# Decoding float64 weights in an attention, experts and SwiGLU kernel: the sign bit cleared on ScalarE, and one epsilon addition for two heads

## Chip, cores and metric

The kernel is one program on one core of a Trainium2 chip. The metric is the device time of one execution in microseconds (us). Lower is better. Three executions were timed without a profiler, and one more was profiled.

## What is computed

Three layers stand behind each other; the first two shapes are (4, 8, 576, 64) per head and (2304, 512) per token.

```python
q_s = softmax(q, axis=-1)                 # with 1e-9 added to each sum
k_s = exp(k - max(k, axis=2)); k_s = k_s / (sum(k_s, axis=2) + 1e-9)
attn = q_s @ (k_s^T @ v)                  # per batch and head
x = attn as (2304, 512)
p = domain_probs / (sum(domain_probs) + 1e-9)
x = sum over e of p[:, e] * (relu(x @ w1[e]) @ w2[e])         # 4 experts, 512 -> 1024 -> 512
out = (silu(x @ w_gate) * (x @ w_val)) @ w_out                # 512 -> 1536 -> 512
```

The three weights of the last layer arrive as float64; everything else is float32. The kernel turns the float64 words into float32 by integer and float operations on their two 32-bit halves, which is called the decode below.

## The kernel before, in words

**Tiling.** The 2304 tokens are worked in two halves, and each half in two blocks X (512 tokens) and Y (640 tokens). A step is one unit of 256 hidden columns for one block. An expert step makes the hidden tile `g` of its unit with seven products instead of eight, each product three matmuls on a high and a low part (`mm3`, L109 to L111, output tiles `h`), turns it into a high and a low part `hh` (ScalarE, L638) and `hl` (VectorE, L643), and in the next step multiplies it with the second weight into tiles `o` of 128x512 (L693 to L695), which VectorE adds to the running sum `acc` (L704). Between the seven products, banks are copied out by ScalarE (`sn`, L503) and combined by VectorE (L509, L518, L524). `weave` lays the `o` tiles between the products.

**What lies between the steps.** In the steps of the first half, attention for batches 2 and 3 runs as a generator (`attend`) on a PSUM bank of its own, "at": column maxima (`ktp`, `mx`, `kmb`), the product of keys and values (`kvp`), transposes of the queries (`qtp`, split into `qT` on ScalarE and VectorE by L104 and L105) and their product `x`. All of these tiles take turns in the bank "at", so that a later one waits until the earlier one has been read. Around the 500th microsecond the kernel turns from the first half to the second.

**The decode.** 36 pieces of 128x512 numbers (`DEC`), two buffers `r` in turn. `decode_load` (L548) loads a piece, 17 positions (about two steps) ahead of its use. `decode` has three stages, placed every two positions: L558 on ScalarE turns the low words into float; L559 on VectorE masks the sign bit off the high words and writes the copy `c`; L561 clamps `c` as float32; then L563 shifts, L564 puts the sign back, L566 adds the low part; the result is stored to DRAM and loaded again when its step comes.

**The attention's key side.** `att_kv` ends with the product `kvp` of 128 rows (two heads of 64) by 130 columns: for each of the two heads 64 columns of values and one column of ones, which gives the sum over the keys. L236 adds epsilon to this sum for the 64 rows of each head, L237 takes the reciprocal, L240 and L241 scale by it. It is called 16 times, with 32 instructions of L236.

**What sets the order.** From step 2 on, the instructions of TensorE and ScalarE stand in the order in which the code is written (`ordered`). Those of VectorE, GpSimd and of the queue of transfers (SyncE) are put in order by a scheduler that works with estimated times; so is everything ahead of step 2. Each engine then works through its list strictly in order.

Of the kernel before, what the change touches and what calls it, by code (L numbers as in the profile page):

```python
# [10 lines left out]
F32 = mybir.dt.float32  # L11
# [3 lines left out]
AF = mybir.ActivationFunctionType  # L15
ALU = mybir.AluOpType
# [3 lines left out]
EPS = 1e-9  # L20
# [7 lines left out]
def attention_experts_swiglu(ctx: ExitStack, tc: tile.TileContext, q, k, v, probs, w1, w2, wg, wv, wo, out):  # L28
# [12 lines left out]
    nc = tc.nc  # L41
    B, H, S, D = q.shape
# [13 lines left out]
    GH = 2  # L56
# [20 lines left out]
    def sbt(tag, shape, name, dt=F32):  # L77
        return sb.tile(shape, dt, tag=tag, name=name, bufs=BUFS[tag])
# [4 lines left out]
    def ps(tag, name):  # L83
        if tag in TURNS:
            TURNS[tag].append(TURNS[tag].pop(0))
            tag = TURNS[tag][0]
        return psp[-1].tile([P, 512], F32, tag=tag, name=name, bufs=BUFS[tag])
# [12 lines left out]
    def f32(ap):  # L100
        return ap.bitcast(F32)
# [15 lines left out]
    def store_later(dst, src):  # L117
        later.append((now[0], dst, src))
# [57 lines left out]
    def load_q(b, g, qt):  # L176
        h = slice(g * GH, (g + 1) * GH)
        nc.sync.dma_start(qt, q[b, h, 0:SM, :].rearrange("h (p c) d -> p h c d", c=C))
        nc.sync.dma_start(rests[b, g][RQ], q[b, h, SM:S, :].rearrange("h r d -> r h d"))
        qin[b, g] = (qt, rests.pop((b, g)))  # L180
# [3 lines left out]
    def W(z):  # L184
        return WAITS[z]

    def att_kv(b, g, tag, tag_m, tag_kv, bank):


        nm = f"{b}{g}"  # L190
        kt, vt, kr, vr = kin.pop((b, g))
        m = sbt(tag_m, [P, 2, P], f"m{nm}")
        kc = kt.rearrange("p h c d -> p c h d")
        nc.vector.tensor_tensor(m.rearrange("p c (h d) -> p c h d", h=GH), kc[:, 0:2], kc[:, 2:4], ALU.max)
        yield W(0), False
        tp = ps(bank, f"ktp{nm}")[:, :2 * P + SR]
        for c in range(2):
            nc.tensor.transpose(tp[:, c * P:(c + 1) * P], m[:, c], ident)
        nc.tensor.transpose(tp[:, 2 * P:], kr[R].rearrange("p h d -> p (h d)"), ident[R, R])
        yield W(1), True  # L200
        mx = sbt("ti", [P, 1], f"mx{nm}")
        nc.vector.tensor_reduce(mx, tp, AX.X, ALU.max)
        yield W(2), False
        mb = ps(bank, f"kmb{nm}")[:, :P]
        nc.tensor.matmul(mb, mx.to_broadcast([P, P]), ident, start=True, stop=True)
        yield W(3), True
        es = sbt(tag, [P, 2, C, GH, D], f"e{nm}") if isinstance(tag, str) else tag
        ek, eqs[b, g] = es[:, 0], es[:, 1]
        mbv = mb.rearrange("p (h d) -> p h d", h=GH)
        nc.vector.tensor_tensor(  # L210
            ek.rearrange("p c h d -> p h c d"), kt, mbv[:, :, None, :].to_broadcast([P, GH, C, D]), ALU.subtract
        )
        nc.vector.tensor_tensor(kr[R], kr[R], mbv[R], ALU.subtract)
        if (b, g) in rests:
            load_q(b, g, kt)
        nc.scalar.activation(ek, ek, AF.Exp)
        nc.scalar.activation(kr[R], kr[R], AF.Exp)
        yield W(4), False
        o = ps(bank, f"kvp{nm}")[:, :GH * D1]
        for c in range(C):  # L220
            nc.tensor.matmul(  # L221
                o, ek[:, c].rearrange("p h d -> p (h d)"), vt[:, c].rearrange("p h d -> p (h d)"),
                start=c == 0, stop=False,
            )
        nc.tensor.matmul(
            o, kr[R].rearrange("p h d -> p (h d)"), vr[R].rearrange("p h d -> p (h d)"), start=False, stop=True
        )
        yield W(5), True
        rs = sbt("ti", [P, 1], f"rs{nm}")
        ov = o.rearrange("p (z e) -> p z e", z=GH)  # L230
        kk = sbt(tag_kv, [P, 2, P], f"kk{nm}", F32R)
        kh, kl = kk[:, 0], kk[:, 1]
        nc.gpsimd.memset(f32(kk), 0.0)
        for z in range(GH):
            zz = slice(z * D, (z + 1) * D)
            nc.vector.tensor_scalar_add(rs[zz], ov[zz, z, D:], EPS)  # L236
        nc.vector.reciprocal(rs, rs)  # L237
        for z in range(GH):
            zz = slice(z * D, (z + 1) * D)
            nc.scalar.activation(kh[zz, zz], ov[zz, z, 0:D], AF.Copy, scale=rs[zz])  # L240
            nc.vector.scalar_tensor_tensor(kl[zz, zz], ov[zz, z, 0:D], rs[zz], f32(kh)[zz, zz], ALU.mult, ALU.subtract)  # L241
        kvs[b, g] = (kh, kl)
        yield W(6), False
# [89 lines left out]
    def attend(groups, bank):  # L333
# [4 lines left out]
        def softmaxes():  # L338
            for z, (b, g) in enumerate(groups):
                while done[0] < z - 1:  # L340
                    yield 1, False
                load_kv(b, g, "kv", "rs")
                yield 4, False
                for wait in att_kv(b, g, "kv", "sm", "sm", bank):
                    yield wait
                for wait in att_q(b, g, nc.vector):
                    yield wait
                done[1] += 1
# [204 lines left out]
    def decode(n):  # L553
        what, f, z = DEC[n]
        r = r64.pop(n)
        rv = r[:, 0:2 * NE].rearrange("p (n b) -> p n b", b=2)
        lo, hi, c = rv[:, :, 0], rv[:, :, 1], r[:, 2 * NE:]
        nc.scalar.activation(lo, lo.bitcast(U32), AF.Copy, scale=2.0 ** -29)  # L558
        nc.vector.tensor_scalar(c, hi, 0x7FFFFFFF, None, ALU.bitwise_and)  # L559
        cf = c.bitcast(F32)  # L560
        nc.vector.tensor_scalar(cf, cf, LEAST, MOST, ALU.max, ALU.min)  # L561
        yield
        nc.vector.tensor_scalar(c, c, 3, 0x3FFFFFF8, ALU.logical_shift_left, ALU.bitwise_and)  # L563
        nc.vector.scalar_tensor_tensor(c, hi, -0x40000000, c, ALU.bitwise_and, ALU.bitwise_or)  # L564
        yield
        nc.vector.tensor_tensor(c, c, lo, ALU.add)  # L566
        if (what, f) not in w32:
            w32[what, f] = dram.tile([P, 2 * NE], F32, tag=f"w32_{what}{f}", name=f"w32_{what}{f}")
        store_later(w32[what, f][:, z * NE:(z + 1) * NE], cf)
        yield  # L570
# [212 lines left out]
    if True:  # L783
# [41 lines left out]
        def start(n):  # L825
            dec[n] = decode(n)
            next(dec[n])
# [6 lines left out]
        for n in range(len(DEC)):  # L834
            z = DEC0 + n * DEC1
# [151 lines left out]
        for b in range(2):  # L987
            for g in range(G):
                chains[f"K{b}{g}"] = att_kv(b, g, e_of[b][g], "sn", kk_of[b][g], kv_bank[b][g])
                chains[f"Q{b}{g}"] = att_q(b, g, QENG[b * G + g])  # L990
                for z in range(2):
                    xb = kv_bank[0][g % 2 * 2 + z] if b == 0 else ("at", "hB")[z]
                    chains[f"X{b}{g}{z}"] = att_x(b, g, z, xb, b == 0)
# [42 lines left out]
```

## Time and profile before

| what | value |
|---|---|
| median of three timed executions | 1337.72 us (1336.94 to 1338.19) |
| profiled execution, its own time | 1339.92 us |
| span of the profiled execution, first to last instruction | 1338.1 us |
| TensorE busy | 1284.3 us, 96% |
| VectorE busy | 966.3 us, 72% |
| ScalarE busy | 598.1 us, 45% |
| GpSimd busy | 562.8 us, 42% |
| mean granted TensorE clock | 0.983 of full speed |

The profiled execution took 1.8 us more than its span, which lies ahead of the first and behind the last instruction. Busy shares are means over stages with different limits. PE is TensorE, DVE is VectorE, ACT is ScalarE, POOL is GpSimd and SPq the queue that issues transfers; PEclk is the granted TensorE clock as a share of full speed; Lnnn is a line of the kernel.

### The profile page before, as it was taken

Reading aid. Unit: us, or ns where it says so; the run is one execution under the profiler, and the core shown is the slowest. Engines: PE = TensorE matmul, PEld = TensorE weight load, DVE = VectorE, ACT = ScalarE, POOL = GpSimd, SP = SyncE. Lnnn points to the kernel's source line nnn. Section 1 sums busy time; section 2 is a strip of 40 time slices with the busy share of each in tenths; the row PEclk is TensorE's granted clock in tenths of the full one; section 3 lists DMA queues with packets and bytes.
Section 4 is the critical chain, followed back from the end, with each engine's and each line's share of the span. In section 5 each row is a group of like instructions: output and inputs, shape, how many; then the busy total and the mean of one; then the engine's idle time right before and its main releaser. Section 6 shows DMA issues by size and latency. Waiting matters only on the chain.

```text
span 1338.1 us, 20294 instructions
## 1 busy us (share of the span) xinstructions
PE 1284.3 (96%) x7568; PEld 1147.2 (86%) x7568; DVE 966.3 (72%) x1634; ACT 598.1 (45%) x1316; POOL 562.8 (42%) x587
## 2 busy tenths in 40 slices
PE   5889999999999998999999999999999999999998
PEld 3678888888888887888888888898988899999997
DVE  6886778778778889677787877555677766666665
ACT  4654334444344444434444343345444544444442
POOL 4753433443254435443545434353444444333420
PEclk9689999999999999999999999999999999999999
DMA  9311423433323334134444432463144247111102
GB/s 206 86 54 40 148 74 102 130 96 92 113 95 112 107 113 157 69 135 129 145 145 154 131 107 72 150 208 117 64 163 155 97 137 254 55 48 48 48 1 71
DMA packets 111298, 148.15 MB, mean 111 GB/s; under 512 B 30560, under 2 KB 71520, under 8 KB 111200
## 3 DMA queue, kind: packets, MB, share of 16 engines
q1 hardware_dynamic: 111200, 146.87, 34.8%
q8 instruction: 59, 0.97, 0.3%
q14 instruction: 39, 0.32, 0.1%
HBM read 109.09 MB, written 37.75 MB: 110 GB/s over the span
## 4 chain that ended last, share of the span: by engine, by line
PE 78%; DVE 10%; DMA 5%; ACT 2%; issue 2%; SPq 1%; POOL 1%; DVEq 0%; POOLq 0%; ACTq 0%
PE o L693 11%; PE o L695 11%; PE o L694 11%; PE h L109 7%; PE h L110 7%; PE h L111 7%; PE h_1g L109 2%; PE h_1g L111 2%; PE h_1g L110 2%; PE h_1v L109 2%; PE h_1v L110 2%; PE h_1v L111 2%; DMA r<-in_moe_w_gate_dram 2%; PE kvp L221 2%; PE h_0v L109 1%
## 5 line engine op out<-in xcount | busy, mean ns | idle before, releaser
L693 PE MATMUL o<-oh,hh 128*128 128x512 f32 x792 | 315.7, 399 | 3.0 <-DVE acc L704 1.5
L695 PE MATMUL o<-oh,hl 128*128 128x512 f32 x792 | 314.6, 397 | 2.5 <-DVE hl L643 2.3
L694 PE MATMUL o<-ol,hh 128*128 128x512 f32 x792 | 312.4, 394 | 0.0
L704 DVE SCALAR_TENSOR_TENSOR acc<-o,pn,acc 128x512 f32<-128x512 f32 x270 | 200.6, 745 | 73.2 <-PE o L695 72.5
L503 ACT COPY sn<-h 128x256 f32<-128x256 f32 (+1 forms) x192 | 76.2, 397 | 253.0 <-PE h L111 252.4
L695 PEld LDWEIGHTS o<-oh,hl 128*128 128x128 f32 x792 | 148.9, 188 | 39.6 <-DVE hl L643 4.2
L638 ACT ACTIVATE hh<-g 128x512 fp32r<-128x512 f32 (+1 forms) x176 | 119.4, 686 | 130.7 <-DVE g L524 73.5
L693 PEld LDWEIGHTS o<-oh,hh 128*128 128x128 f32 x792 | 149.1, 188 | 22.6 <-DVE acc L704 1.7
L694 PEld LDWEIGHTS o<-ol,hh 128*128 128x128 f32 x792 | 148.9, 188 | 17.2
L643 DVE SCALAR_TENSOR_TENSOR hl<-g,hh 128x512 fp32r<-128x512 f32 (+1 forms) x128 | 109.2, 855 | 31.5 <-ACT hh L638 28.7
L708 DVE TENSOR_TENSOR acc<-o,acc 128x512 f32<-128x512 f32 x90 | 61.9, 688 | 45.9 <-PE o L695 44.8
L521 ACT COPY g<-h 128x256 f32<-128x256 f32 (+1 forms) x64 | 25.6, 400 | 89.4 <-PE h L111 89.3
L645 DVE TENSOR_TENSOR hl<-g,hh 128x512 fp32r<-128x512 f32 (+1 forms) x48 | 48.6, 1012 | 3.2 <-ACT hh L638 2.4
L559 DVE TENSOR_SCALAR r<-r 128x512 int32<-128x512 int32 x36 | 23.1, 642 | 30.6 <-DMA r<-in_moe_w_val_dram 11.7
L105 POOL TENSOR_TENSOR xo<-xp,xo 128x256 fp32r<-128x256 f32 (+1 forms) x24 | 22.4, 935 | 52.5 <-ACT xo L104 47.2
L662 ACT ACTIVATE g<-g 128x512 f32<-128x512 f32 (+1 forms) x48 | 33.0, 688 | 21.0 <-DVE g L524 21.0
L524 DVE TENSOR_TENSOR g<-h,sn 128x256 f32<-128x256 f32 (+1 forms) x64 | 29.0, 453 | 17.9 <-PE h L111 17.5
L503 ACT COPY sn_1g<-h_1g 128x320 f32<-128x320 f32 x36 | 15.4, 427 | 56.2 <-PE h_1g L111 56.1
L518 DVE TENSOR_TENSOR g<-h,sn 128x256 f32<-128x256 f32 (+1 forms) x64 | 28.9, 451 | 9.7 <-ACT sn L503 9.5
L566 DVE CUSTOM_DVE_ANT_0 r<-r 128x1024 uint16<-128x1024 uint16 x36 | 32.0, 889 | 3.1 <-ACT r L558 3.0
L509 DVE TENSOR_TENSOR g<-h,sn 128x256 f32<-128x256 f32 (+1 forms) x64 | 28.8, 451 | 3.7 <-PE h L111 2.3
L564 DVE SCALAR_TENSOR_TENSOR r<-r 128x512 int32<-128x512 int32 x36 | 31.0, 862 | 0.7
(1174 smaller groups left out, 3857.1 us busy)
## 6 DMA issues: line engine op xcount, KB each, us to landing
pd<-xo SPq DMA_DIRECT2D x28, 320.0 KB, 2.8
pd<-xo SPq DMA_DIRECT2D x28, 256.0 KB, 2.5
r<-in_moe_w_gate_dram SPq DMA_DIRECT2D x12, 512.0 KB, 4.3
r<-in_moe_w_val_dram SPq DMA_DIRECT2D x12, 512.0 KB, 4.6
r<-in_moe_w_out_dram SPq DMA_DIRECT2D x12, 512.0 KB, 4.0
xl<-pd SPq DMA_DIRECT2D x14, 320.0 KB, 5.3
xh<-pd SPq DMA_DIRECT2D x14, 320.0 KB, 5.3
out_dram<-acc SPq DMA_DIRECT2D x16, 256.0 KB, 2.3
```

Source lines behind the costliest of these rows:

```text
L109: nc.tensor.matmul(o, wh, xh, start=first, stop=False, skip_group_check=more)
L110: nc.tensor.matmul(o, wh, xl, start=False, stop=False, skip_group_check=more)
L111: nc.tensor.matmul(o, wl, xh, start=False, stop=last, skip_group_check=more)
L503: nc.scalar.copy(sn[z], banks[0])
L638: nc.scalar.activation(hh[:, :, t * n:(t + 1) * n], g[:, :, t], AF.Relu if kind == "e" else AF.Copy)
L643: nc.vector.scalar_tensor_tensor(hl[:, :, ts], g[:, :, t], 0.0, f32(hh[:, :, ts]), ALU.max, ALU.subtract)
L645: nc.vector.tensor_tensor(hl[:, :, ts], g[:, :, t], f32(hh[:, :, ts]), ALU.subtract)
L693: nc.tensor.matmul(p, hh[:, z, ts], w[z][0], start=z == 0, stop=False)
L694: nc.tensor.matmul(p, hh[:, z, ts], w[z][1], start=False, stop=False)
L695: nc.tensor.matmul(p, hl[:, z, ts], w[z][0], start=False, stop=z == NF - 1)
L704: nc.vector.scalar_tensor_tensor(o, p, weight, o, ALU.mult, ALU.add)
L708: nc.vector.tensor_tensor(o, p, o, ALU.add)
```

## The change

Two edits. The mask of the sign bit, an integer operation on VectorE, becomes an absolute value on ScalarE: it reads the high words as float32 and writes the same copy `c`. And since each row of `kvp` holds its own key sum in the column of ones of either head, the two additions of epsilon on 64 rows become one on 128 rows, which reads the first head's column.

```diff
@@ att_kv
         nc.gpsimd.memset(f32(kk), 0.0)
-        for z in range(GH):
-            zz = slice(z * D, (z + 1) * D)
-            nc.vector.tensor_scalar_add(rs[zz], ov[zz, z, D:], EPS)
+        nc.vector.tensor_scalar_add(rs, ov[:, 0, D:], EPS)
         nc.vector.reciprocal(rs, rs)
@@ decode
         nc.scalar.activation(lo, lo.bitcast(U32), AF.Copy, scale=2.0 ** -29)
-        nc.vector.tensor_scalar(c, hi, 0x7FFFFFFF, None, ALU.bitwise_and)
         cf = c.bitcast(F32)
+        nc.scalar.activation(cf, hi.bitcast(F32), AF.Abs)
         nc.vector.tensor_scalar(cf, cf, LEAST, MOST, ALU.max, ALU.min)
         yield
```

Lines behind the first edit move up by two. In the changed kernel the decode reads: L556 low words and L558 absolute value, both ScalarE; L559 clamp, L561 shift, L562 sign, L564 addition, all VectorE (before: L561, L563, L564, L566). Likewise L704 becomes L702, L643 L641, L518 L516, L524 L522, L509 L507, L503 L501, L638 L636. L105 and L210 keep their numbers.

Through the scheduler the first edit also moves the rest of the decode on VectorE. The first place is VectorE's list around one of the eight column maxima of attention in the first half, the one whose bank "at" is freed by the VectorE read L105 `qT` (L210 is the first reader of the tile `kmb` that takes the bank next). Before:

```order
L704 SCALAR_TENSOR_TENSOR acc_68<-o_1_2_3595,pn,acc_68 128x512
L559 TENSOR_SCALAR r_1_1560<-r_1_1560 128x512
L561 TENSOR_SCALAR r_1_1560<-r_1_1560 128x512
L563 TENSOR_SCALAR r_1_1560<-r_1_1560 128x512
L564 SCALAR_TENSOR_TENSOR r_1_1560<-r_1_1560 128x512
L524 TENSOR_TENSOR g_0_3499<-h_01_3529,sn_02_3568 128x256
L105 TENSOR_TENSOR qT_3631<-qtp_3615,qT_3631 128x256
```

With the change, the same place:

```order
L702 SCALAR_TENSOR_TENSOR acc_68<-o_1_2_3582,pn,acc_68 128x512
L522 TENSOR_TENSOR g_0_3486<-h_01_3516,sn_03_3576 128x256
L641 SCALAR_TENSOR_TENSOR hl_0_3488<-g_0_3486,hh_0_3487 128x2x256
L105 TENSOR_TENSOR qT_3618<-qtp_3602,qT_3618 128x256
L702 SCALAR_TENSOR_TENSOR acc_68<-o_1_3_3605,pn,acc_68 128x512
L210 TENSOR_TENSOR e_3652<-kv_3432,kmb_3630 128x2x4x64
```

The four decode instructions of piece 11 (`r_1`) are gone from here. They now stand in VectorE's list about two steps later, behind piece 11's two instructions on ScalarE. Before, this second place held only the last of the five, L566:

```order
L643 SCALAR_TENSOR_TENSOR hl_0_3800<-g_0_3798,hh_0_3799 128x2x256
L704 SCALAR_TENSOR_TENSOR acc_68<-o_1_4_3921,pn,acc_68 128x512
L566 ISA r_1_1560<-r_1_1560 128x1024
L509 TENSOR_TENSOR g_1_3936<-h_12_3958,sn_11_3946 128x320
L105 TENSOR_TENSOR qT_3982<-qtp_3969,qT_3982 128x320
L704 SCALAR_TENSOR_TENSOR acc_67<-o_0_0_3985,pn,acc_67 128x512
```

With the change:

```order
L641 SCALAR_TENSOR_TENSOR hl_0_3786<-g_0_3784,hh_0_3785 128x2x256
L559 TENSOR_SCALAR r_1_1551<-r_1_1551 128x512
L702 SCALAR_TENSOR_TENSOR acc_68<-o_1_4_3907,pn,acc_68 128x512
L561 TENSOR_SCALAR r_1_1551<-r_1_1551 128x512
L507 TENSOR_TENSOR g_1_3922<-h_12_3944,sn_11_3932 128x320
L562 SCALAR_TENSOR_TENSOR r_1_1551<-r_1_1551 128x512
L105 TENSOR_TENSOR qT_3968<-qtp_3955,qT_3968 128x320
L564 ISA r_1_1551<-r_1_1551 128x1024
L702 SCALAR_TENSOR_TENSOR acc_67<-o_0_0_3971,pn,acc_67 128x512
```

All four instructions that the change leaves on VectorE stand together here, with other work between them. All 36 pieces move in this way. The third place is ScalarE's list at piece 25, where a bank copy stands right behind the decode. Before:

```order
L638 ACTIVATE hh_1_6712<-g_1_6711 128x2x320 x2
L558 ACTIVATE r_1_1560<-r_1_1560 128x512
L503 COPY sn_01_6837<-h_00_6830 128x256
L104 CAST xo_6840<-xp_6530 128x256
L104 CAST oh_6862<-raw22o 128x512
```

With the change:

```order
L636 ACTIVATE hh_1_6696<-g_1_6695 128x2x320 x2
L556 ACTIVATE r_1_1551<-r_1_1551 128x512
L558 ACTIVATE r_1_1551<-r_1_1551 128x512
L501 COPY sn_01_6821<-h_00_6814 128x256
L104 CAST xo_6824<-xp_6514 128x256
L104 CAST oh_6846<-raw22o 128x512
```

The absolute value stands between the low words and the bank copy. ScalarE's list has two table loads (ACT_TABLE_LOAD) in all, in both kernels and at the same two places.

## Rows read from the trace of the kernel before

**Rows 1.** Windows: length, busy us (count) of PE, PEld, DVE, ACT, POOL; PEclk, DMA.

```profile
140.00:480.00 340.00, 333.37 (x1932) 293.95 (x1931) 267.41 (x478) 145.41 (x319) 136.71 (x150) 0.99 0.35 107
480.00:540.00 60.00, 52.51 (x299) 45.63 (x298) 52.42 (x76) 28.86 (x59) 30.54 (x25) 0.97 0.42 135
540.00:840.00 300.00, 299.08 (x1738) 267.52 (x1737) 225.67 (x358) 128.56 (x276) 138.43 (x129) 1.00 0.38 122
```

**Rows 2.** Waits of PE, 130 to 480 us: total, times, longest.

```profile
PE kmb L205 <- DVE qT L105: 5.0, 2, 3.0
PE h L109 <- DVE g L518: 1.0, 2, 0.6
PE o L695 <- DVE hl L643: 0.3, 1, 0.3
```

**Rows 3.** Waits of PE, 480 to 540 us; last row: the one of 540 to 860.

```profile
PE o L695 <- DVE hl L643: 2.0, 1, 2.0
PE h L109 <- DVE g L518: 1.6, 2, 1.3
PE o L693 <- DVE acc L704: 1.5, 1, 1.5
...
PE h L109 <- DVE g L518: 0.7, 1, 0.7
```

**Rows 4.** Chain that ended last, 155.0 to 163.2 us: start, length, what.

```profile
155.60 4.56 DMA r<-in_moe_w_val_dram
...
160.26 0.43 DVE r L559
...
162.16 0.46 PE kmb L205 x2
```

**Rows 5.** The same chain, 339 to 351 us.

```profile
339.16 5.85 DMA r<-in_moe_w_out_dram
...
345.14 1.32 DVE r L559
...
348.36 0.69 DVE r L564
...
349.86 0.46 PE kmb L205 x2
```

**Rows 6.** Windows of 3.4 us: behind each stop, and one at full clock.

```profile
162.90:166.30 3.40, 3.40 (x14) 3.27 (x13) 2.22 (x5) 1.15 (x3) 0.00 (x0) 0.50 0.85 250
166.40:169.80 3.40, 3.40 (x22) 3.12 (x21) 2.61 (x6) 0.43 (x1) 0.00 (x0) 1.00 0.30 84
350.70:354.10 3.40, 3.40 (x14) 3.30 (x13) 2.41 (x5) 1.15 (x3) 0.00 (x0) 0.51 0.26 92
```

**Rows 7.** DVE groups by form, 130 to 860 us: busy, mean ns | idle before, releasers.

```profile
L559 DVE TENSOR_SCALAR r<-r 128x512 int32<-128x512 int32 x36 | 23.1, 642 | 30.6 <-DMA r<-in_moe_w_val_dram 11.7 <-DMA r<-in_moe_w_gate_dram 10.9 <-DMA r<-in_moe_w_out_dram 8.0
L566 DVE CUSTOM_DVE_ANT_0 r<-r 128x1024 uint16<-128x1024 uint16 x36 | 32.0, 889 | 3.1 <-ACT r L558 3.0
```

**Rows 8.** Instructions of three lines: duration ns min/median/max, first and last start.

```profile
L558 ACT ACTIVATE r<-r x36: 653/672/696, 151.8 to 832.1; 128x512 int32<-128x512 uint32 x36
L559 DVE TENSOR_SCALAR r<-r x36: 410/428/1524, 149.8 to 804.2; 128x512 int32<-128x512 int32 x36
L236 DVE TENSOR_SCALAR rs<-kvp x32: 140/156/164, 23.8 to 452.5; 64x1 f32<-64x1 f32 x32
```

**Rows 9.** Timeline of ACT and PE at pieces 25 and 14: start, length, [idle before].

```profile
654.92 0.67 ACT L558 ACTIVATE r<-r 128x512 int32<-128x512 uint32 x1
655.48 0.35 ACT L503 COPY sn<-h 128x256 f32<-128x256 f32 x1
657.36 0.28 PE L109 MATMUL h<-xh,wh22a 128*128 128x256 f32 x1
...
439.12 0.43 ACT L503 COPY sn<-h 128x320 f32<-128x320 f32 x1 [1.37 <-PE h L111]
```

**Rows 10.** Chain that ended last in the turn, 498 to 513 us.

```profile
502.07 0.56 ACT r L558
```

## The prediction

> **What bounds the kernel now.** I read first the busy time by stage. In the first half, TensorE is busy 333.4 of 340 us and VectorE 267.4; in the turn 52.5 of 60 and 52.4; in the second half 299.1 of 300 and 225.7 [rows 1]. So TensorE bounds, and only its idle time can be won. The waits of TensorE show where that idle time lies. From 130 to 480 us they come to 6.3 us, of which 5.0 are two stops of the matmul `kmb` behind VectorE's read of `qT` [rows 2]. The turn holds three waits on VectorE of 5.1 us together and some smaller ones, and from there to 860 us there is one of 0.7 us [rows 3]. Behind 860 us nothing is decoded, and the change moves nothing there.
>
> Next I read what VectorE was doing ahead of the two stops. The chain of waits says the same both times: a load of `r` lands, the mask L559 runs, then work that has nothing to do with it, then `qT`, then `kmb` [rows 4, 5]. L559 stands in VectorE's list ahead of `qT`, and its piece has not landed. The scheduler, it seems, took the load to be quicker than it is. Over all 36 pieces VectorE stood idle 30.6 us ahead of L559, every time on a load [rows 7]. Most of this costs nothing, because TensorE has other tiles to work on; twice it cost a stop.
>
> A stop costs more than its length. The granted clock in the 3.4 us behind each one is 0.50 and 0.51, the lower of the two levels (1.2 of 2.4 GHz), after TensorE had stood still for 2 and 3 us; just after, it is 1.00 again. In that stretch 14 matmuls start instead of 22 [rows 6]. Eight of 22 in 3.4 us is 1.2 us for each stop.
>
> **The change, part by part.**
>
> *The mask goes from VectorE.* 36 instructions, 23.1 us busy, and 30.6 us of waiting ahead of them [rows 7]. The busy time by itself is worth nothing where VectorE has slack. What counts is that the instruction which waits for the load leaves VectorE's list, and that the three behind it leave that place too: as the order shows, clamp, shift and sign now stand about two steps later, behind ScalarE's two instructions for the same piece. At the second stop the load lands at 345.0 us (339.16 + 5.85), and four decode instructions, from L559 to L564, then run until 349.05 [rows 5] ahead of the one that reads `qT`. With the change none stands there. At the first stop piece 2's mask and piece 1's burst are gone; piece 0's burst stands there in their stead, earlier, and has no load to wait for. So both stops go: 5.0 us of waiting and 2 x 1.2 us of slow clock, 7.4 us.
>
> The other waits outside the turn come to 1.0 + 0.3 + 0.7 = 2.0 us [rows 2, 3]. Some stand behind a decode burst and some behind VectorE's general load; bounds 0 and 2.0, I take half, 1.0.
>
> *The absolute value comes to ScalarE.* No absolute value was traced. The nearest row is L558, which reads the same buffer with the same step and writes 128x512: 672 ns [rows 8]; the bounds are its 653 and 696. 36 x 0.67 = 24.1 us on an engine that is busy 145 of 340 us in the first half [rows 1]. No table load is added. Its load is in the buffer long before: ScalarE comes to the last piece at 832.1 us, where VectorE's mask ran at 804.2 as soon as the load was there [rows 8]. If the addition L566, whose end frees the buffer for the next load, slips by the 3 us or so of the burst now ahead of it, those 28 us are hardly touched. Behind it on ScalarE stands whatever the step copies next. I went through all 36 places in the timeline: at 20 of them ScalarE idles over 0.67 us before its next instruction, as the 1.37 us at piece 14, and the absolute value fits in. At the other 16 the next instruction is pushed, up to 0.67 us, as at piece 25, where the copy L503 starts while L558 drains. There the copy ends at 655.83 and the product that needs its bank starts at 657.36 [rows 9], a lead of 1.5 us, so TensorE should not see it. Cost with that cover 0; without it 16 x 0.67 = 10.7 us.
>
> *The clamp now waits for ScalarE.* Behind it on VectorE stand bank reads such as L518 and evictions. How long it waits isn't in the trace; the nearest row is L566, which the scheduler placed behind L558 in the same manner, and which waited in 5 of 36 cases, 3.0 us in all [rows 7]. The bounds are 0 and 36 x 0.6 = 21.6 us of VectorE's time. I take about the 3.0 us that L566 now no longer pays: no difference.
>
> *The burst in its new place.* Four instructions of 0.4 to 1.5 us stand together ahead of an addition or a bank read. Before, three or four of them stood together as well, so the length is no news, only the place. Of the eight `kmb` places in the order, three have a burst within two steps ahead; the timeline of before has time to spare at two of them and almost none at the third. I take 0.7 us of new waits, between 0 and one whole new stop of 2.5 + 1.2 us.
>
> *The turn.* There the chain that ended last runs through L558 on ScalarE to the weight casts [rows 10], so one absolute value lies on the path: 0.7 us lost. Against it, shift and sign of piece 18 no longer stand ahead of the addition for which TensorE waited 1.5 us [rows 3]. Net 0.8 us won, between -0.7 and 5.1.
>
> *The epsilon.* 16 instructions of 156 ns go [rows 8], 2.5 us of VectorE. The instruction on 128 rows should take as long as that on 64, since the elements per row are the same. Most calls lie under TensorE's work; those of the start, where VectorE sets the pace, may give 0.3 us (0 to 2.5).
>
> **Sum.** 7.4 + 1.0 + 0.8 + 0.3 - 0.7 = 8.8 us. The profiled execution took 1339.9 us, which would become 1331.1. The median of the timed runs stands 2.2 us lower, at 1337.7; I take the same saving from it: 1328.9, so 1329.
>
> **The rivals.**
>
> *The turn opens too.* If all three waits on VectorE there go (5.1 us instead of 1.5), with a slow stretch of clock that follows one of them, and all of the 2.0 us outside, the gain is near 15 us: 1318 to 1325. For it: VectorE is at its fullest there, 52.4 of 60 us [rows 1]. Against it: what fills it there is the preparation of the next half, and that stays.
>
> *The wait comes back as a wait for ScalarE.* If every clamp waits 0.6 us, 21.6 of the 30.6 us are back, and by that measure 8.8 x 9.0 / 30.6 = 2.6 us of gain are left: 1335. Against it: L566 waited in 5 cases only.
>
> *ScalarE's copies come late.* If each of the 16 pushes reaches TensorE, 10.7 us eat the gain: 1339.6. Against it speaks the lead of 1.5 us. The Trainium skill, page "ScalarE: Activation LUTs", section "Rules for kernel authors", says that simple functions such as relu, max and min belong on VectorE and not on ScalarE. By that rule the move is a loss. The rows agree that the single instruction gets dearer (672 against 428 ns at the median [rows 8]), but which engine waits for what is not in the rule.
>
> *The burst stops `kmb` elsewhere* (the other sign). The same mechanism as now, at another place: a burst ahead of `qT`, TensorE standing still 2.5 us and 1.2 us of slow clock behind it, 3.7 us each. One or two such stops leave a gain; from four on, 14.8 us, the kernel is slower than before: 1343.7. For it: the two stops of now were as unforeseen. Against it: the bursts no longer begin with a load that is late.
>
> **How the numbers follow.** The forecast (1325 to 1333) gets 0.62, the open turn 0.10, the wait for ScalarE (1333 to 1338) 0.15, the late copies 0.05, the new stops 0.08. A measurement here can tell about 0.2%, 2.7 us, so faster means under 1335.0 and slower above 1340.4. Faster: 0.62 + 0.10 + 0.04 of the wait for ScalarE = 0.76. Slower: 0.07 of the new stops and 0.02 of the late copies = 0.09. The rest, 0.15, is no difference. The range goes from 1322, in the middle of the open turn, to 1337, in the upper part of the wait for ScalarE.
>
> **What would show it.** After the change the waits of TensorE from 130 to 480 us should hold no wait of `kmb` over 1 us, and no stretch at half clock there. VectorE should wait for no load of `r`; the clamp should wait for ScalarE a few microseconds in all. The absolute value should take 0.65 to 0.70 us. The turn should stay at 7 us of waits or so. The forecast is wrong if the start changes by more than 2 us, since the scheduler also reorders it and I have no row that prices that; if a new stop appears at one of the `kmb` places; or if the two stops belong to the profiled execution and not to the timed ones.

## The result, and the profile after

The changed kernel takes 1325.89 us (median of 4, 1324.73 to 1330.49) against 1337.45 us for the kernel before beside it (4 runs): a ratio of 0.9912 [0.9884, 0.9941], 11.6 us by the medians. A second measurement gave 0.9906 [0.9886, 0.9926]. The forecast was 1329.0 us, a gain of 8.8. By the profiled executions it is 14.0 us (1339.92 to 1325.93), but the one of before ran 2.5 us above its median, and the second profile of the changed kernel took 1328.14 us.

Windows of the changed kernel, with the columns of [rows 1]:

```profile
140.00:480.00 340.00, 338.95 (x1992) 300.54 (x1991) 258.44 (x462) 159.92 (x347) 140.75 (x156) 1.00 0.36 111
480.00:540.00 60.00, 54.27 (x311) 47.21 (x310) 50.27 (x71) 30.01 (x62) 28.85 (x24) 0.97 0.39 123
540.00:840.00 300.00, 300.00 (x1749) 269.12 (x1749) 227.06 (x349) 138.72 (x293) 142.74 (x134) 1.00 0.37 120
```

In the first half TensorE is idle for 1.0 us of 340 instead of 6.6 [rows 1], and starts 1992 matmuls in it instead of 1932. The second half has no idle time left. The turn is nearly as it was.

The waits of TensorE, 140 to 480 us (first row) and 480 to 540 us (the others), which answer to [rows 2, 3]:

```profile
PE o L691 <- DVE acc L702: 0.8, 1, 0.8
...
PE h L109 <- DVE g L516: 3.7, 2, 2.5
PE h L110 <- POOL xl L105: 0.8, 1, 0.8
PE o L693 <- DVE hl L641: 0.6, 1, 0.6
PE o L691 <- ACT xt L408: 0.6, 1, 0.6
```

Both stops of `kmb` are gone, and from 540 to 860 us no wait is left. (L691 was L693, L408 was L410.)

The chain that ended last, at the place of the second stop, 341.1 to 342 us:

```profile
341.11 0.16 PE h L110
341.27 0.46 PE kmb L205 x2
341.73 0.23 PE o L691
```

Where before a load, the mask and three more decode instructions led up to `kmb` [rows 5], the chain is now TensorE's own: `kmb` follows the matmul ahead of it without a gap. The clock stays up behind it; two windows of 3.4 us, behind either place of `kmb` (158.8 and 341.3 us):

```profile
158.90:162.30 3.40, 3.40 (x24) 3.23 (x23) 2.93 (x6) 1.58 (x4) 0.46 (x2) 1.00 0.83 236
341.30:344.70 3.40, 3.40 (x23) 3.27 (x24) 3.18 (x6) 1.52 (x4) 0.69 (x2) 1.00 0.46 125
```

24 and 23 matmuls at 1.00 stand where it was 14 at 0.50 and 0.51 [rows 6].

The instructions of the absolute value and the clamp (duration in ns: least, median, most; first and last start; who waited for them, us and times):

```profile
L558 ACT ACTIVATE r<-r x36: 641/660/678, 151.1 to 818.2; 128x512 f32<-128x512 f32 x36
  DVE r L559: 3.3, 10
...
L559 DVE TENSOR_SCALAR r<-r x36: 412/428/1532, 151.8 to 819.7; 128x512 f32<-128x512 f32 x36
```

**Where the gain lies.** ScalarE's conversion of the low words is the first instruction of each piece, its order on ScalarE is fixed from step 2 on, and it comes 36 times; its start times serve as landmarks. Its first and last starts were 151.8 and 832.1 us [rows 8] and are now:

```profile
L556 ACT ACTIVATE r<-r x36: 649/669/683, 150.6 to 817.7; 128x512 int32<-128x512 uint32 x36
```

So the kernel is 1.2 us ahead when the decode begins and 14.4 ahead when it ends. The table says in which stretch each kernel wins (minus) or loses time against the profiled execution of before: the shift of a landmark less that of the one before it. Piece 0 to 1 holds the first stop, 9 to 10 the second, 16 to 20 is the turn.

| us | start to 0 | 0 to 1 | 1 to 9 | 9 to 10 | 10 to 16 | 16 to 20 | 20 to 35 | 35 to end | sum |
|---|---|---|---|---|---|---|---|---|---|
| the change | -1.2 | -3.8 | -1.0 | -4.5 | -1.5 | -0.9 | -1.7 | +0.5 | -14.0 |
| the change again | -0.7 | -3.8 | -1.0 | -4.5 | -1.6 | +0.1 | -1.7 | +1.2 | -11.8 |
| sign only | -0.7 | -3.8 | -0.7 | -4.5 | -1.5 | -1.0 | -1.7 | +1.2 | -12.7 |
| epsilon only | +2.2 | -1.6 | +0.2 | -0.2 | -0.2 | +0.3 | +0.1 | +2.1 | +2.9 |
| mask behind ScalarE | -2.0 | -2.7 | -0.4 | -4.5 | -1.3 | -1.1 | +1.2 | +0.8 | -10.1 |
| mask and absolute value | -1.9 | -1.8 | -1.2 | -3.1 | -0.9 | -0.5 | -0.8 | 0.0 | -10.0 |
| absolute value twice | +0.6 | -3.3 | -0.6 | -4.5 | -1.0 | +0.1 | 0.0 | +0.7 | -7.9 |
| pieces 0 to 15 | -2.0 | -2.7 | -0.9 | -4.5 | -0.1 | +1.2 | -0.3 | +1.4 | -8.0 |
| pieces 16 to 35 | -2.3 | -1.6 | +1.0 | +0.1 | -1.0 | -0.9 | -1.7 | -0.2 | -6.6 |
| no sign at all | +3.0 | -2.0 | 0.0 | -0.6 | 0.0 | -0.9 | +0.8 | +0.2 | +0.4 |

Each row is one execution. The start moves by 5 us in all from kernel to kernel, in both directions. Where the change itself is run again, the stretches between the pieces repeat to 0.1 us outside the turn; the turn differs by 1.0 us and the end by 0.7.

### The profile page after: what moved, and what is told of

Its sections match the earlier page's. It is cut to its first block, busy times and chain, and to the rows that moved or that the text cites. A ratio compares the mean times of both kernels' runs of the same rounds, so it can differ in the third digit from the quotient of the medians.

```text
span 1324.2 us, 20265 instructions
## 1 busy us (share of the span) xinstructions
PE 1277.1 (96%) x7568; PEld 1142.7 (86%) x7568; DVE 947.7 (72%) x1582; ACT 617.8 (47%) x1352; POOL 563.3 (43%) x587
## 4 chain that ended last, share of the span: by engine, by line
PE 86%; DVE 5%; POOL 3%; ACT 2%; DMA 1%; issue 1%; SPq 1%; POOLq 0%; DVEq 0%; ACTq 0%
PE o L691 13%; PE o L693 13%; PE o L692 13%; PE h L109 9%; PE h L110 9%; PE h L111 8%; PE h_1g L109 2%; PE h_1g L111 2%; PE h_1g L110 2%; PE h_1v L109 2%; PE h_1v L110 2%; PE h_1v L111 2%; PE h_0v L109 1%; PE h_0v L111 1%; PE h_0v L110 1%
## 5 line engine op out<-in xcount | busy, mean ns | idle before, releaser
L691 PE MATMUL o<-oh,hh 128*128 128x512 f32 x792 | 315.9, 399 | 1.9 <-ACT xt L408 1.1
L693 PE MATMUL o<-oh,hl 128*128 128x512 f32 x792 | 313.5, 396 | 0.7 <-DVE hl L641 0.6
L702 DVE SCALAR_TENSOR_TENSOR acc<-o,pn,acc 128x512 f32<-128x512 f32 x270 | 200.8, 744 | 93.5 <-PE o L693 92.4
L501 ACT COPY sn<-h 128x256 f32<-128x256 f32 (+1 forms) x192 | 76.3, 398 | 244.4 <-PE h L111 244.0
L693 PEld LDWEIGHTS o<-oh,hl 128*128 128x128 f32 x792 | 148.9, 188 | 36.6 <-DVE hl L641 1.1
L636 ACT ACTIVATE hh<-g 128x512 fp32r<-128x512 f32 (+1 forms) x176 | 119.3, 685 | 106.7 <-DVE g L522 49.4
L691 PEld LDWEIGHTS o<-oh,hh 128*128 128x128 f32 x792 | 149.1, 188 | 21.9 <-ACT xt L408 1.6
L641 DVE SCALAR_TENSOR_TENSOR hl<-g,hh 128x512 fp32r<-128x512 f32 (+1 forms) x128 | 114.2, 893 | 34.0 <-ACT hh L636 30.5
L643 DVE TENSOR_TENSOR hl<-g,hh 128x512 fp32r<-128x512 f32 (+1 forms) x48 | 48.5, 1011 | 3.2 <-ACT hh L636 2.4
L522 DVE TENSOR_TENSOR g<-h,sn 128x256 f32<-128x256 f32 (+1 forms) x64 | 28.9, 452 | 25.9 <-PE h L111 25.5
L105 POOL TENSOR_TENSOR xo<-xp,xo 128x256 fp32r<-128x256 f32 (+1 forms) x24 | 22.3, 929 | 50.4 <-ACT xo L104 45.3
L501 ACT COPY sn_1g<-h_1g 128x320 f32<-128x320 f32 x36 | 15.4, 427 | 56.3 <-PE h_1g L111 56.2
L516 DVE TENSOR_TENSOR g<-h,sn 128x256 f32<-128x256 f32 (+1 forms) x64 | 29.0, 452 | 16.2 <-ACT sn L501 16.1
L562 DVE SCALAR_TENSOR_TENSOR r<-r 128x512 int32<-128x512 int32 x36 | 35.2, 976 | 0.3
L564 DVE CUSTOM_DVE_ANT_0 r<-r 128x1024 uint16<-128x1024 uint16 x36 | 30.9, 859 | 0.3
L672 DVE TENSOR_TENSOR g<-g,v 128x512 f32<-128x512 f32 (+1 forms) x24 | 22.1, 923 | 11.5 <-ACT v L519 11.4
L507 DVE TENSOR_TENSOR g<-h,sn 128x256 f32<-128x256 f32 (+1 forms) x64 | 28.6, 447 | 1.7 <-ACT wh2a L104 0.9
```

Source lines behind the costliest of these rows:

```text
L501: nc.scalar.copy(sn[z], banks[0])
L636: nc.scalar.activation(hh[:, :, t * n:(t + 1) * n], g[:, :, t], AF.Relu if kind == "e" else AF.Copy)
L641: nc.vector.scalar_tensor_tensor(hl[:, :, ts], g[:, :, t], 0.0, f32(hh[:, :, ts]), ALU.max, ALU.subtract)
L643: nc.vector.tensor_tensor(hl[:, :, ts], g[:, :, t], f32(hh[:, :, ts]), ALU.subtract)
L691: nc.tensor.matmul(p, hh[:, z, ts], w[z][0], start=z == 0, stop=False)
L693: nc.tensor.matmul(p, hl[:, z, ts], w[z][0], start=False, stop=z == NF - 1)
```

## The experiments

The theory: the gain comes from which engine's list the late load stops. The chief rival: VectorE has 23 us less to do, and that is the gain. Line numbers in the rows are those of each kernel. The diffs are excerpts, of `decode` unless said otherwise. The first two are against the kernel before, the third is against the kernel with the epsilon alone, the others are against the changed kernel.

**Either edit alone.** First the sign:

```diff
         nc.scalar.activation(lo, lo.bitcast(U32), AF.Copy, scale=2.0 ** -29)
-        nc.vector.tensor_scalar(c, hi, 0x7FFFFFFF, None, ALU.bitwise_and)
         cf = c.bitcast(F32)
+        nc.scalar.activation(cf, hi.bitcast(F32), AF.Abs)
```

> The sign edit alone, with the two epsilon additions of before. Theory 1 (VectorE no longer waits for the load of a piece ahead of other work): nearly the whole gain of the change, 10 to 12 us faster than before, no stop of the matmul kmb over 1 us. Rival (the epsilon edit and the reordering of the start that it brings carry a good part): under 8 us faster.

Measured: 0.9918 [0.9905, 0.9931], 1327.89 us. This is the whole gain. Then the epsilon, in `att_kv`:

```diff
-        for z in range(GH):
-            zz = slice(z * D, (z + 1) * D)
-            nc.vector.tensor_scalar_add(rs[zz], ov[zz, z, D:], EPS)
+        nc.vector.tensor_scalar_add(rs, ov[:, 0, D:], EPS)
```

> The epsilon edit alone, with the mask on VectorE as before. Theory 1: within 2 us of before, at most 1 us faster; VectorE again idles about 30 us ahead of the mask, and the two stops of kmb of 2 to 3 us stand again. Rival: 3 us or more faster.

Measured: 1.0021 [1.0007, 1.0035], 1340.97 us: not faster, but slower by 0.2%, a little more than the 2 us that I allowed. In its profile the stops stand as before; rows of the waits of TensorE and of VectorE:

```profile
PE kmb L205 <- DVE qT L105: 4.9, 2, 3.0
...
DVE r L557 <- DMA r<-in_moe_w_val_dram: 15.0, 9, 3.2
```

By the table it loses 2.2 us in the start and 2.1 behind the decode, and the stretch of the first stop is 1.6 us shorter, though that stop stands. What the 1.6 us are comes with the clock below.

**The mask kept on VectorE, but placed behind ScalarE.** ScalarE first writes 8 of the 512 columns of `c`, which the mask then overwrites. So VectorE does all its work of before, but the mask has to wait for ScalarE's step and no longer stands where the load is late.

```diff
         nc.scalar.activation(lo, lo.bitcast(U32), AF.Copy, scale=2.0 ** -29)
+        nc.scalar.activation(c[:, 0:8], lo[:, 0:8].bitcast(U32), AF.Copy, scale=2.0 ** -29)
         nc.vector.tensor_scalar(c, hi, 0x7FFFFFFF, None, ALU.bitwise_and)
```

> Epsilon as changed, the mask kept on VectorE, but a ScalarE instruction on 8 columns behind the low words' one writes into the copy first, so that the mask cannot stand ahead of it in VectorE's list. The output is the reference's. VectorE keeps all of its 36 masks (16 to 23 us busy). Theory 1 (the place of the mask counts, not the engine): 9 to 13 us faster than before, as the change. Rival theory 2 (VectorE's work, less by 23 us, is what gave the time): under 4 us faster.

Measured: 0.9943 [0.9924, 0.9962], 1329.51 us, a gain of 7.6 us by the ratio, between the two expectations but nearer to the theory's. Waits of TensorE (130 to 480 us, then 480 to 540) and of VectorE:

```profile
PE kmb L205 <- DVE qT L105: 0.9, 1, 0.9
...
PE h L109 <- DVE g L516: 5.0, 2, 4.5
...
DVE r L558 <- ACT r L557: 7.0, 8, 1.2
```

No wait for a load of `r` is left, and the second stop is gone in full (-4.5 us). The first leaves 0.9 us, but no load and no decode stands ahead of it: `hl`, just ahead of `qT`, takes 1.78 us there, and 0.68 with the change (second row):

```profile
156.71 1.78 DVE L642 SCALAR_TENSOR_TENSOR hl<-g,hh 128x512 fp32r<-128x512 f32 x1
...
157.47 0.68 DVE L641 SCALAR_TENSOR_TENSOR hl<-g,hh 128x512 fp32r<-128x512 f32 x1
```

Most of what the change gains on top of this lies behind piece 20, +1.2 instead of -1.7 us: there TensorE waits 1.5 us for VectorE's bank reads, in three waits, and not at all with the change. So the place is most of the gain. That the rest is VectorE's work is not shown: ahead of two of these three matmuls TensorE waits in the kernel with two absolute values as well (below), where VectorE does no more than with the change.

**The change, with the mask on VectorE as well.** The mask writes the copy early as before, and ScalarE overwrites it with the absolute value:

```diff
         nc.scalar.activation(lo, lo.bitcast(U32), AF.Copy, scale=2.0 ** -29)
         cf = c.bitcast(F32)
+        nc.vector.tensor_scalar(c, hi, 0x7FFFFFFF, None, ALU.bitwise_and)
         nc.scalar.activation(cf, hi.bitcast(F32), AF.Abs)
```

> The change, and the mask of before in addition: VectorE writes the masked copy, ScalarE then writes the same values over it. The mask stands early in VectorE's list again and waits for the load, but clamp, shift and sign stay late. The output is the reference's. Theory 1, as far as the waiting alone counts: about 30 us of VectorE idle ahead of the mask come back, the second stop comes back with 0.5 to 1.5 us instead of 3, and 1 to 5 us of the gain are lost. If the burst behind the mask did the harm and not its wait: under 1 us lost. Theory 2 (VectorE's work): all of the gain lost.

Measured: 0.995 [0.9938, 0.9962], 1332.01 us: 4 to 5 us of the gain are lost. Waits of TensorE and of VectorE:

```profile
PE kmb L205 <- DVE qT L105: 2.2, 2, 1.4
...
DVE r L558 <- DMA r<-in_moe_w_val_dram: 10.3, 8, 2.6
DVE r L558 <- DMA r<-in_moe_w_out_dram: 9.3, 7, 2.8
DVE r L558 <- DMA r<-in_moe_w_gate_dram: 4.6, 5, 1.7
```

With 24.2 us of waiting for loads on VectorE again, the second stop is back with 1.4 us instead of 3.0: load, mask, `g`, `hl` and `qT` stand in its chain, and clamp, shift and sign no longer do. The 0.8 us at the first place are not the mask's: no load ends last there, and `hl` takes 1.72 us, much as in the kernel with the mask behind ScalarE.

**No clearing of the sign at all.** The run that tells the two apart most sharply: the clamp reads the raw high word on VectorE, so that VectorE has 36 instructions less than before and ScalarE none more, but the instruction that waits for the load is VectorE's. What it leaves out is the size of negative weights, which the clamp sets to its lower bound.

```diff
-        nc.scalar.activation(cf, hi.bitcast(F32), AF.Abs)
-        nc.vector.tensor_scalar(cf, cf, LEAST, MOST, ALU.max, ALU.min)
+        nc.vector.tensor_scalar(cf, hi.bitcast(F32), LEAST, MOST, ALU.max, ALU.min)
```

> The change without any clearing of the sign: the clamp on VectorE reads the raw high word (negative weights are clamped to the lower bound; that part of the computation is left out). 36 instructions less than before on VectorE (23 us), none more on ScalarE, but the instruction that waits for the load of r is VectorE's again, and stands ahead of qT at both places. Theory (what counts is whose queue the late load stops): the stops of kmb are back, 3 to 5 us, and with them most of the gain goes: ratio 0.995 to 0.999, 3 to 9 us slower than the change although it does less work. Rival (VectorE's load counts): as fast as the change or faster, ratio 0.988 to 0.992.

Measured: 0.9987 [0.9967, 1.0007], 1339.02 us, no difference from before. VectorE is busy 946.3 us, as little as with the change (947.7), and nothing is won. (Its profile starts 3.0 us late; from piece 0 to 35 it gains 2.7 us by the table, but 1.6 of these are the clock behind the first stop, see below. So the smaller load is worth some 1 us there.) The chain that ended last at the second place:

```profile
340.15 5.31 DMA r<-in_moe_w_out_dram
...
345.59 0.44 DVE r L558
...
346.05 1.42 DVE r L560
...
347.50 1.66 DVE r L561
349.15 0.33 DVE g L522
349.49 0.60 DVE hl L640
350.09 0.34 DVE qT L105
...
350.57 0.56 PE kmb L205 x2
```

It is the chain of [rows 5] with one decode instruction less: the load lands, and the decode runs ahead of `qT`. TensorE waits for it again, and the clamp waits for loads as the mask did [rows 7]; waits of TensorE, then the clamp's group on VectorE (busy, mean ns | idle before):

```profile
PE kmb L205 <- DVE qT L105: 3.9, 2, 2.4
...
L558 DVE TENSOR_SCALAR r<-r 128x512 f32<-128x512 f32 x36 | 20.8, 577 | 33.0 <-DMA r<-in_moe_w_val_dram 13.5 <-DMA r<-in_moe_w_gate_dram 10.7 <-DMA r<-in_moe_w_out_dram 8.7
```

**Which pieces.** The absolute value for pieces 0 to 15 alone, then for 16 to 35 alone, and the mask for the others:

```diff
-        nc.scalar.activation(cf, hi.bitcast(F32), AF.Abs)
+        if n < 16:
+            nc.scalar.activation(cf, hi.bitcast(F32), AF.Abs)
+        else:
+            nc.vector.tensor_scalar(c, hi, 0x7FFFFFFF, None, ALU.bitwise_and)
```

> Absolute value on ScalarE for pieces 0 to 15 alone; pieces 16 to 35 keep the mask on VectorE. Theory (the gain is the two stops and the small waits of the first half): 10.5 to 12 us are won, ratio 0.991 to 0.9925, and the landmark at piece 16 stands as early as with the change (some 11 to 12 us). Rival (the gain comes from VectorE's lower load all along): no more than 16/36 of it, some 5 us, ratio 0.996.

> The other half: mask on VectorE for pieces 0 to 15, absolute value on ScalarE for pieces 16 to 35. Theory: both stops at kmb stay (5.0 us of waits with the slow clock behind them), and 1 to 3 us are won from the turn on, ratio 0.998 to 0.999. Rival (lower load): 20/36 of the gain, some 6 us, ratio 0.995.

Measured: 0.9956 [0.9941, 0.9971] and 0.9978 [0.9961, 0.9994]. The second is as expected: its gain in the turn and behind it, 0.9 and 1.7 us, is the change's own to 0.1 us, and the stops stand. The first is worth less than expected, 5.9 us by its ratio instead of 10.5 to 12, and by that number alone the rival (some 5 us) did better. Its stretches speak for the theory: 8.2 us are won from piece 0 to 16 and none behind it. The second stop is gone, but a wait of 0.8 us is left at the first (`hl` takes 1.72 us there too), the 1.5 us of pieces 10 to 16 don't come, and the turn loses 1.2 us. Why these go the other way isn't shown; the scheduler places VectorE's instructions anew when the forms are mixed. (The profiled execution ran 2.9 us below its kernel's median.) The two parts together (5.9 + 2.9 us) make 8.8 of the 12.

**ScalarE's slack.** The absolute value twice, in place:

```diff
         nc.scalar.activation(cf, hi.bitcast(F32), AF.Abs)
+        nc.scalar.activation(cf, cf, AF.Abs)
```

> The change as it is, with the absolute value taken a second time on ScalarE in place (36 x 0.66 = 23.8 us more of ScalarE; the output stays the reference's, since a second absolute value changes nothing). Theory: ScalarE has slack and the clamp has time, so the time stays within 2 us of the changed kernel's (ratio to before about 0.991 to 0.993), and the clamp waits for ScalarE some 5 to 12 us in all instead of 3.3, without TensorE seeing it. Rival (ScalarE's copies come late): the pushes of the next copies double from 0.66 to 1.3 us and reach TensorE, 5 to 11 us of the gain are lost (ratio 0.995 to 0.999).

Measured: 0.9946 [0.9927, 0.9964], 1331.39 us. My theory is wrong here: 4 to 5 us of the gain are lost, the lower end of what the rival gave. The clamp waits for ScalarE hardly more than with the change (3.9 us against 3.3). The second instruction takes 0.63 us. From the landmark of piece 0 on, this kernel falls behind the change by 1.4 us up to piece 16, 1.0 in the turn and 1.6 up to piece 35, 4.0 in all. It is not a little at each piece: matched matmul by matmul with the change, nearly all of it outside the turn stands at five places, 0.3 to 0.7 us each. At two of them (1.0 us) a copy of ScalarE comes last, once right behind the second absolute value, as the rival had it (first three rows). At the other three (1.9 us) it is VectorE, which has no more to do than with the change, but does it in another order, or with a slow `hl` (last row, one of the two matmuls that wait with the mask behind ScalarE too):

```profile
557.14 0.63 ACT r L559
557.78 0.27 ACT sn L501
558.09 0.39 PE h L109
...
583.86 0.38 PE L109 MATMUL h<-xh,wh19a 128*128 128x256 f32 x1 [0.40 <-DVE g L516]
```

So only a third of that loss is ScalarE's lateness. The largest wait of the turn is now for a copy of ScalarE, where with the change it was for VectorE (2.5 us):

```profile
PE h L109 <- ACT g L519: 4.1, 1, 4.1
```

**The clamp on GpSimd**, an attempt to go on along the same way:

```diff
-        nc.vector.tensor_scalar(cf, cf, LEAST, MOST, ALU.max, ALU.min)
+        nc.gpsimd.tensor_scalar(cf, cf, LEAST, MOST, ALU.max, ALU.min)
```

> The change, with the clamp on GpSimd instead of VectorE as well: 18.9 us leave VectorE, 36 instructions go to an engine that is 43% busy (its nearest row, two inputs of 128x512, takes 1170 ns). If what is left of VectorE's load still costs TensorE something (the turn's two waits of 3.7 us, first of all), 1 to 3 us are won over the change: ratio 0.989 to 0.991. Theory: only what waits in a queue ahead of a matmul counts and little of that is left, so within 2 us of the change; slower by up to 5 us if GpSimd's splits of x stand behind a clamp that waits for ScalarE.

Measured: 1.0227 [1.0204, 1.025], 1369.33 us, 30 us slower than before, where I had expected at most 5 us more than with the change. The clamp's own row with what it waits for and who waits for it, and TensorE's waits, 140 to 480 and 540 to 840 us:

```profile
L559 POOL TENSOR_SCALAR r<-r x36: 1908/1917/2852, 156.2 to 863.0; 128x512 f32<-128x512 f32 x36
...
  ACT r L558: 53.7, 13
...
  DVE r L561: 63.0, 30
```

```profile
PE h L109 <- DVE g L516: 10.2, 7, 3.5
...
PE h L109 <- DVE g L516: 11.4, 9, 2.9
```

The clamp takes 1.92 us there instead of 0.43, and the shift, which stays on VectorE, waits for it 63 us in all. Behind the shift stand the bank reads L516, and TensorE waits for them. It is the mechanism of the two stops once more, made large: 18.9 us leave VectorE, and its list stops for twice as long as it did ahead of the mask (30.6 us [rows 7]).

**No decode in the turn.** The change, with pieces 17 to 35 decoded 24 positions later; and then with a piece every 11 positions (where the pieces are placed, outside `decode`):

```diff
-            z = DEC0 + n * DEC1
+            z = DEC0 + n * DEC1 + (24 if n >= 17 else 0)
```

```diff
-            z = DEC0 + n * DEC1
+            z = 51 + 11 * n if n < 18 else 282 + 11 * (n - 18)
```

> The change, with pieces 17 to 35 decoded 24 positions later, so that none is decoded in the turn. Theory (VectorE and ScalarE are fullest there, and what is left of TensorE's waits between 480 and 540 us, 5.7 us, stands behind decode work): 1 to 4 us are won over the change, ratio 0.988 to 0.991. Rival (the turn's waits come from the preparation of the next half): no difference from the change, or 1 to 3 us lost because the last pieces now fall into the SwiGLU steps behind 820 us.

> As the run before, but with a piece every 11 positions instead of 12, 18 pieces ahead of the turn and 18 behind it, so that the last piece is decoded as early as with the change. Theory: the pieces now fall on other places of the steps, one more of them ahead of qT, and ScalarE's work falls on other copies; the turn's 1 to 4 us are won if that costs nothing: ratio 0.988 to 0.991. Rival (the places matter more than the turn): slower than the change by 2 to 8 us.

Beside them the change ran once more:

> The changed kernel once more, beside the three below, on the same chip. Theory and rivals alike: ratio 0.991 to 0.993, and a profile without a stop of kmb over 1 us between 140 and 480 us.

Measured: 0.9917 [0.9898, 0.9935] and 0.9918 [0.9896, 0.994], the change beside them 0.9906 [0.9886, 0.9926]. No difference, where 1 to 4 us were expected; the rival of the first run was right. VectorE's busy time from 480 to 540 us falls from 50.3 to 45.4 us in the first of the two, and TensorE still waits 7.5 us there; the largest of its waits:

```profile
PE h L109 <- DVE g L516: 3.2, 2, 2.7
PE o L693 <- DVE hl L641: 1.3, 1, 1.3
PE h L109 <- ACT sn L501: 0.8, 1, 0.8
...
```

So taking the decode out of the turn doesn't remove the waits there. No version beats the change.

## Why the prediction was right, point by point

The forecast of 1329 us came 3 us too high. The mechanism was right; most of the difference is in one term, the small waits.

**The two stops, 7.4 us.** Right, and a little too small: -3.8 and -4.5 us in the stretches that hold them, 8.3 in all. The mis-sized part is the price of the slow clock, 1.2 us a stop by the count of matmuls started. Three kernels price it directly. In the profiles with the epsilon alone, with pieces 16 to 35 and with no sign, the first stop stands, but the clock behind it stayed at 1.00, and the second stop has its slow stretch. Windows behind the two stops of the kernel with pieces 16 to 35:

```profile
160.00:163.40 3.40, 3.40 (x23) 3.23 (x23) 3.38 (x8) 1.58 (x4) 0.00 (x0) 1.00 0.88 290
347.40:350.80 3.40, 3.40 (x13) 3.11 (x13) 2.68 (x6) 0.35 (x2) 0.00 (x0) 0.51 0.31 111
```

With the same 5.0 us of waiting for `kmb` as before, its stretch from piece 0 to 1 is 1.6 us shorter than before, as it is with the epsilon alone: a slow stretch costs 1.6 us. That is why "stop gone" reads -3.8 us for 2.0 us of waiting, and why part of the profiled 14.0 us may belong to the execution of before that was profiled: how many of its timed executions had that slow stretch isn't known.

**The cause: a load that lands late, in VectorE's list.** Shown for the place of the decode in that list. Less work on VectorE with the wait left there gives nothing (0.9987); all the work with the wait taken from there gives 7.6 us; the change with the early mask put back loses 4 to 5. The prediction named two parts, the late load and the three instructions behind the mask, and the second stop shows both: with the load and the mask alone 1.4 us of its 3.0 are back, and the rest stays away with clamp, shift and sign. At the first stop no run parts the two. From 7.6 us to the change's 12 some 4 us are left, of which the rows above put 0.9 down to a slow `hl` and most of the rest to waits for VectorE behind piece 20; whether VectorE's work or its order makes these, no run parts in full.

**Other waits outside the turn, half of 2.0 us = 1.0; the burst in its new place, 0.7 lost.** These are the terms that were most off. All of those waits went, not half, and the burst made no new one (the 0.8 us for `acc` is what is left of the 1.5 us in the turn [rows 3], which now falls ahead of 480 us): -1.0, -1.5 and -1.7 us in the stretches 1 to 9, 10 to 16 and 20 to 35, together 4.2 against the 0.3 of the sum. Why this is twice the 2.0 us of waits that [rows 2, 3] list comes out when the matmuls of both profiles are matched one by one: the 4.2 us stand at seven places, each behind a read or `hl` of VectorE. One of them, before and with the change:

```profile
388.97 0.40 PE L695 MATMUL o<-oh,hl 128*128 128x512 f32 x1
389.78 0.41 PE L109 MATMUL h<-xh,wh11a 128*128 128x320 f32 x1 [0.41 <-DVE g L518]
...
378.55 0.40 PE L693 MATMUL o<-oh,hl 128*128 128x512 f32 x1
378.79 0.31 PE L109 MATMUL h<-xh,wh11a 128*128 128x320 f32 x1
```

The list counts 0.41 us from the end of the matmul ahead. Without the wait, the next one starts 0.24 us behind the start of that matmul, before its end; so the wait costs 0.57 us, and 0.10 more at the matmul behind it. Three of the seven waits are too short for the list. One of these has a late load and the mask L559 in its chain, as the stops have. That all these waits went is half of the rival "the turn opens too"; its other half, the turn, did not come.

**The turn, 0.8 us.** The size holds for one profile (-0.9) and not for the other (+0.1), and where it holds it is luck. The absolute value does lie on the path, as forecast; a row of the chain that ended last, 484 to 500.8 us:

```profile
489.97 0.56 ACT r L558
```

But of the 1.5 us at the addition only 0.7 came; the 0.8 us left are the wait for `acc` that now falls ahead of 480 us. The rest is larger than either and stood in no term. There is one more wait for VectorE before, behind the dots of [rows 3], about as long as those that the prediction counts:

```profile
PE xtp L409 <- DVE acc L702: 1.4, 1, 1.4
```

With the change that wait is gone, the one for `hl` falls from 2.0 to 0.6 us, and those for `g` grow from 1.6 to 3.7. The waits were to stay at some 7 us and came to 6.5 with the one for `acc`. That the preparation of the next half fills the turn, as the prediction said, agrees with the runs without decode in it.

**The epsilon, 0.3 us.** No gain: by itself the kernel is 0.2% slower (1.0021), and beside the sign it makes no difference (0.9912 against 0.9918). One instruction on 128 rows takes as long as one on 64 did, as assumed (152 against 156 ns at the median). The 1.2 us of the start are not its work: the sign alone starts 0.7 us earlier, and kernels that share the epsilon edit lie between 2.3 us earlier and 3.0 later there. Why the start moves so stays open; the scheduler orders it anew in every kernel, and no run here kept it fixed. Behind piece 35, where nothing was to move, the two profiles lose 0.5 and 1.2 us.

**The absolute value, 0.67 us, no cost on ScalarE.** 0.66 us, and with one of them TensorE has no wait for a copy of ScalarE in the first half. In the turn it is on the path (above). The margin is not as wide as the lead of 1.5 us at piece 25 suggested: with a second one a copy is late for TensorE by 0.3 us right behind it. Whether the first costs something of this sort that the gain hides isn't shown.

**The clamp's wait for ScalarE, some 3.0 us.** 3.3 us, 10 times, and outside the turn TensorE waits for nothing behind it.

The rule of the Trainium skill (page "ScalarE: Activation LUTs", section "Rules for kernel authors") gives simple functions such as relu, max and min to VectorE. The rows bear out its price, 660 against 428 ns at the median, and the outcome goes the other way, because a place in a list was worth more here than the instruction.

The clamp took 4.5 times as long on GpSimd as on VectorE (1917 against 428 ns). The Trainium skill, page "GPSIMD Engine Reference", section "3.1 Elementwise — side-by-side cycle accounting", gives a ratio of 1.96 for an addition of two float32 inputs; the clamp is another instruction with one input, and for it the measurement decides.

## What to carry to other kernels

Look at what an instruction waits for and what stands behind it in its engine's list before looking at what it costs: where a scheduler places the first reader of a load too early, that reader stops everything behind it, and giving the reader (not just any work) to an engine whose order is fixed and later can gain even if it gets dearer there. Test this by leaving out the work and keeping the wait; if next to nothing is won, the work was not the cost. Before pricing waits from a list of idle times, match the matmuls of two profiles start by start: here the list showed half of what the small waits cost. One more instruction per piece on ScalarE went with the whole gain, with a second one 4 to 5 us were lost, and the clamp on GpSimd cost 2.3%, so each such move needs its own measurement.

## What the runs showed of the hardware

The clock behind a stop is not the same each time. The first stop of `kmb`, 1.9 to 2.0 us of waiting in the kernel before, with the epsilon alone and with pieces 16 to 35, was followed by a stretch of 3.4 us at half clock in the first profile and at full clock in the other two; behind the second stop (3.0 us, and 2.4 with no sign) the half clock came in all four profiles where it stands at that length. In the start, stretches at half clock up to 75 us add up to 30.7 us in the profile of before and to 13.7 in that of the change, with the first decode only 1.2 us apart; so the clock cost little there.

An instruction of VectorE doesn't always take the same time. At the second stop of before, mask and clamp took 1.31 and 1.38 us, while GpSimd split `wl11a` (344.87 to 347.58 us), and the shift behind them took 0.43 at 347.89. Of the 36 clamps of that kernel 19 took over 0.6 us, and each of these ran beside arithmetic of GpSimd for more than half of its time; the other 17 did so for 11% of theirs on average. No run here moved GpSimd's work away, so that this is the reason is not shown, and with the change `hl` took 0.68 us beside such a split.
